# T5-bias attention followed by a mixture of adapters: a third of the adapter outputs taken from VectorE, the adapters' weights moved to the sync queue, later inputs loaded by token tiles

## The chip, the core and the metric

The kernel runs on one core of one Trainium2 chip. A core has TensorE (PE, matmuls; its weight loads are shown as PEld), VectorE (DVE), ScalarE (ACT), GpSimd (POOL) and SyncE (SP), each with an instruction stream of its own that runs in order, and 16 DMA engines that serve the queues of SP, ACT and POOL. The metric is the device time of one execution in microseconds, the median over runs.

## What is computed

`q`, `k` and `v` are [8, 8, 576, 64] in fp32 (batch, head, token, dimension). Attention with a T5 position bias gives 8 x 576 = 4608 tokens of 512 numbers. Each token then goes through the two of eight rank-16 adapters that its gate picks, and the result is added to it.

```python
scores = scale * np.matmul(q, k.transpose(0, 1, 3, 2)) + bias   # bias by distance, from a table
attn = softmax(scores)
x = np.matmul(attn, v)            # to [4608, 512]

logits = x @ w_gate               # [4608, 8]
w = softmax over the two largest logits of each token
delta = sum over those two e of w[e] * ((x @ A[e]) @ B[e])
return x + delta
```

## The kernel before

**Units and slots.** The work is cut into 32 units, one for each batch `b` and pair of heads `hp` (four pairs), numbered `u = 4b + hp`. A unit has six slots `s` (0 to 5). A loop over all 192 slots (line 586) writes the instructions of all engines in program order; each engine keeps that order, so an instruction that waits holds up all that stand behind it on its engine. In each slot `scores(u, s)` writes PE's score matmuls into one of two PSUM buffers and ACT's exponential that reads them (lines 256 and 260; line 268 for the last 64 keys). The value matmuls of the unit before (`values`, line 303), the bias multiplications on DVE (`bias`, lines 274 and 285) and, in slot 5, the normalisation on DVE (`normalise`, lines 313 and 314) follow.

**Inputs.** `load(b)` makes a list of DMA issues for one batch: fp32 staging tiles `q32`, `k32`, `v32` ([128 tokens, 4 token tiles, 8 heads, 64]) for tokens 0 to 511, and `qke32`, `ve32` for the last 64 tokens. There are two sets of staging tiles, used by batches in turn. A main load is one head: four token tiles, 128 KB, in pieces of 256 bytes. That makes 28 issues a batch, ordered by pair of heads. The loop pops them from the list onto SP's queue (line 595): three a slot in units 0 and 1, then one or two. The list for batch `b + 2` is made in slot 4 of pair 2 of batch `b` (line 646).

POOL casts the staged data to bf16. For unit `u + 2`, `cast_qk` (line 129) casts q in slot 2 and k in slot 4 of unit `u`; `cast_v` (line 133) casts v of unit `u + 1` in slot 1; `cast_tails` (lines 138 and 139) casts the last tokens of batch `b + 1` in slot 5 of pair 2. PE transposes the q and k of unit `u + 1` (`transpose_pe`, line 224) in slot 0 of unit `u` from unit 4 on, and DVE copies them out (line 228).

**Adapters' weights.** `load_adapters(c)` (line 202) issues six DMAs from POOL in the six slots of unit 3: four 128-row chunks of A and the gate into `AW` (bf16), and B into `Bc` (bf16). The DMA casts from fp32. They are first used by the `zl` matmuls (line 355).

**Adapters.** When a batch's attention is done, `batch_done` puts its token tiles into groups of three (of two for batch 6; batch 7 has a path of its own, class `Last`). A `Group` runs in steps, each a PE part and a part on other engines, which `place` spreads over even slots (slots 0, 2 and 4; slot 5 too in the last two batches): transposes of x, the z matmul and its copy on ACT, the gates on DVE, POOL and ACT, the transposes of the weighted z, and for each token tile `t` the output `dl_pe(t)` and `dl_out(t)`. `dl_out` is DVE's addition of x (line 407) and the store on SP's queue (line 409). `dl` takes one of the two PSUM buffers named `mm`, which the transposes use too. In a queue of steps, the output of tile 1 is followed by `weigh` of the next group (lines 381 to 387).

Of the kernel before, what the change touches and what calls it, by code (L numbers as in the profile page):

```python
# [11 lines left out]
FP32 = mybir.dt.float32  # L12
BF16 = mybir.dt.bfloat16
AX = mybir.AxisListType
ALU = mybir.AluOpType
# [18 lines left out]
def kernel(  # L34
# [11 lines left out]
    nc = tc.nc  # L46
    B, H, S, D = q.shape
    NB = bias_table.shape[0]
    Dm = H * D
    E = moe_w_gate.shape[1]  # L50
    r = moe_A.shape[2]
    ER = E * r
    HP = H // 2
# [15 lines left out]
    cp = ctx.enter_context(tc.tile_pool(name="const", bufs=1))  # L69
# [19 lines left out]
    def load(b):  # L89

        q32 = stg.tile([128, 4, H, D], FP32, name="q32", tag="q32")
        k32 = stg.tile([128, 4, H, D], FP32, name="k32", tag="k32")
        v32 = stg.tile([128, 4, H, D], FP32, name="v32", tag="v32")
        qke32 = stg.tile([128, H, D], FP32, name="qke32", tag="qke32")
        ve32 = stg.tile([128, HP, D], FP32, name="ve32", tag="ve32")
        staged[b] = (q32, k32, v32, qke32, ve32)
        todo = []

        def main(eng, t, src, hp):
            for h in (2 * hp, 2 * hp + 1):  # L100
                todo.append(lambda h=h: eng.dma_start(  # L101
                    out=t[:, :, h, :],
                    in_=src[b, h, :512, :].rearrange("(j p) d -> p j d", p=128)))

        for hp in range(HP):
            second = nc.scalar if b == 0 and hp == 0 else nc.sync
            main(nc.sync, q32, q, hp)
            main(second, k32, k, hp)
            if hp == 0:
                for i, (src, eng) in enumerate(((q, nc.sync), (k, second))):  # L110
                    todo.append(lambda i=i, src=src, eng=eng: eng.dma_start(
                        out=qke32[i * 64:(i + 1) * 64],
                        in_=src[b, :, 512:, :].rearrange("h p d -> p h d")))
            main(nc.sync, v32, v, hp)
            if hp == 0:
                for par in range(2):
                    todo.append(lambda par=par: nc.sync.dma_start(
                        out=ve32[par * 64:(par + 1) * 64],
                        in_=v[b, :, 512:, :].rearrange("(g two) p d -> two p g d", two=2)[par]))
        return deque(todo)  # L120
# [10 lines left out]
    def cast_v(u, eng):  # L131
        b, hp = units[u]
        eng(out=vals[b % 2][0][:, :, 2 * hp:2 * hp + 2, :D],  # L133
            in_=staged[b][2][:, :, 2 * hp:2 * hp + 2, :])
# [52 lines left out]
    ident = cp.tile([128, 128], BF16, tag="ident")  # L187
# [3 lines left out]
    todo = load(0)  # L191
# [7 lines left out]
    AW = cp.tile([128, 4, ER + E], BF16, tag="AW")  # L199
    Bc = cp.tile([ER, Dm], BF16, tag="Bc")  # L200

    def load_adapters(c):
        if c < 4:
            nc.gpsimd.dma_start(out=AW[:, c, :ER].rearrange("p (e r) -> p e r", e=E),
                                in_=moe_A[:, c * 128:(c + 1) * 128, :].rearrange("e d r -> d e r"))
        elif c == 4:
            nc.gpsimd.dma_start(out=AW[:, :, ER:], in_=moe_w_gate.rearrange("(c p) e -> p c e", p=128))
        else:
            nc.gpsimd.dma_start(out=Bc, in_=moe_B.rearrange("e r d -> (e r) d"))


    xs, xe, probs, accs = {}, {}, {}, {}
# [7 lines left out]
    def transpose_pe(u):  # L220
        ps = tps[u] = mp.tile([128, 2, 4, 128], BF16, name="tp", tag="mm")
        for i in range(2):
            for j in range(4):
                nc.tensor.transpose(ps[:, i, j, :], nats[u][:, i, j, :], ident)  # L224
# [15 lines left out]
    def scores(u, s):  # L240
        b, hp = units[u]
        qT, kT = qkT[b][:, hp, 0, :], qkT[b][:, hp, 1, :]
        sc = scp.tile([128, 2, SW], FP32, name="sc", tag="sc")
        if s == 0:
            probs[u] = (ep.tile([128, 2, 4 * S], BF16, name="pm", tag="pm"),
                        ep.tile([128, S], BF16, name="pe", tag="pe"))
        pm, pe = probs[u]
        if s < SLOTS - 1:
            c, end = SW * s, min(SW * (s + 1), 4 * S)
            n = end - c  # L250
            while c < end:
                j, q0 = divmod(c, S)
                w = min(S - q0, end - c)
                for h in range(2):
                    rows = slice(h * 64, (h + 1) * 64)
                    nc.tensor.matmul(sc[:, h, c - SW * s:c - SW * s + w],  # L256
                                     lhsT=kT[rows, j * 128:(j + 1) * 128],
                                     rhs=qT[rows, q0:q0 + w], start=True, stop=True)
                c += w
            nc.scalar.activation(pm[:, :, SW * s:end], sc[:, :, :n], ACT.Exp, scale=scale)  # L260
        else:
            flat = sc.rearrange("p a b -> p (a b)")
            for q0, n in ((0, 512), (512, 64)):
                for h in range(2):
                    rows = slice(h * 64, (h + 1) * 64)
                    nc.tensor.matmul(flat[rows, q0:q0 + n], lhsT=kT[rows, 512:],  # L266
                                     rhs=qT[rows, q0:q0 + n], start=True, stop=True)
            nc.scalar.activation(pe, flat[:, :S], ACT.Exp, scale=scale)  # L268
# [62 lines left out]
    class Group:  # L331
# [67 lines left out]
            nc.vector.tensor_copy(self.zT, self.zps)  # L399

        def dl_pe(self, t):
            self.dl = mp.tile([128, Dm], FP32, name="dl", tag="mm")
            nc.tensor.matmul(self.dl, lhsT=self.zT[:, t, :], rhs=Bc, start=True, stop=True)  # L403

        def dl_out(self, t):
            ot = ms.tile([128, Dm], FP32, name="ot", tag="ot", bufs=4)
            nc.vector.tensor_tensor(ot, self.dl, self.x[t], op=ALU.add)  # L407
            for p0, n0, cnt in self.rows[t]:
                nc.sync.dma_start(out=out[n0:n0 + cnt, :], in_=ot[p0:p0 + cnt, :])

# [175 lines left out]
    for t in range(SLOTS * NU):  # L586
        u, s = divmod(t, SLOTS)
        b, hp = units[u]
        p = u - 1
        scores(u, s)  # L590
        for fn, args in due.pop(t, []):
            fn(*args)
        if u == 3:
            load_adapters(s)
        for i in range(3 if u < 2 else 2 if s % 3 == 0 else 1):
            if loading:
                loading.popleft()()
        early = u >= NU - HP and hp in (0, HP - 1)
        if s == 0:
            if u == 0:  # L600
                while loading:
                    loading.popleft()()
                loading = load(1)
            if p >= 0:
                bias(p, 3)
                if not early:
                    values(p, 0)
            if HP <= u < NU - 1:
                transpose_pe(u + 1)
            place(t + 1)  # L610
        if s == 1:
            if p >= 0:
                bias(p, 4)
                values(p, 1)
            if u + 1 < NU:
                if u >= HP:
                    transpose_out(u + 1)
                cast_v(u + 1, pool_cast)
        if s == 2:
            if p >= 0:  # L620
                values(p, 2)
                if early:
                    values(p, 3)
            if u + 2 < NU:
                cast_qk(u + 2, 0, pool_cast)
            place(t + 1)
        if s == 3:
            if p >= 0:
                values(p, 4 if early else 3)
            bias(u, 0)  # L630
            if early:
                finish(p, t)
        if s == 4:
            if p >= 0 and not early:
                values(p, 4)
            if u + 2 < NU:
                cast_qk(u + 2, 1, pool_cast)
            if u < HP:
                transpose_pe(u + 1)
            if hp == HP - 1 and b + 1 < B:  # L640
                tails_pe(b + 1)
                tails_out(b + 1)
            if hp == 2 and b + 2 < B:
                while loading:
                    loading.popleft()()
                loading = load(b + 2)
            place(t + 1)
        if s == 5:
            if u < HP:
                transpose_out(u + 1)  # L650
            if p >= 0 and not early:
                finish(p, t)
            if hp == 2 and b + 1 < B:
                cast_tails(b + 1, pool_cast)
            bias(u, 1, 2)
            if u in (NU - HP - 1, NU - 2, NU - 1):
                values(u, 0)
            if b >= B - 2:
                place(t + 1)


    u = NU - 1
# [50 lines left out]
```

## Time and profile before

| what | value |
|---|---|
| median of 3 runs | 231.32 us (231.14 to 232.71) |
| the profiled execution's own time | 233.92 us |
| its span in the profile | 231.8 us |
| mean granted TensorE clock | 0.955 |
| loads of q, k, v by head: issues on SP and ACT, median to landing | 192 of 128 KB, 2.9 to 3.1 us |
| adapters' DMAs on POOL (lines 204, 207, 209) | 6 |
| output additions on DVE (line 407) | 31, of 0.68 us |
| copies of the same size from PSUM on ACT (line 561) | 3, of 0.586 us |
| packets of the sync queue, of POOL's queue | 120056, 4832 |

The profile is of one execution. Its page gives each engine's busy time, 40 equal slices of the span, and the DMA queues; other views list instructions in order of time with the idle time of the engine before each and what ended it, the chain of waits that ends with the last instruction, and busy times by stretch. An engine's busy time leaves out its waits and the issuing of DMAs.

### The profile page before, as it was taken

The page shows a single profiled execution, that of the slowest core. Times are in us where ns is not written, and L with a number is a line of the kernel's source. Part 1 is how long each engine was busy: PE and PEld are TensorE (multiplying, and loading weights), DVE is VectorE, ACT ScalarE, POOL GpSimd, SP SyncE. Part 2 cuts the span into 40 slices and gives each one's busy share as a digit, 9 for nine tenths or more (in the row PEclk, how much of TensorE's full clock was granted, in tenths as well). Part 3 has the DMA queues.
Part 4 walks back from the last instruction along what each step waited for, and adds up shares of the span by engine and source line. Part 5 has one row for each costly group of instructions (what it writes and reads, how often), then busy time and mean ns, then how long its engine had stood idle before and what let it go on. Part 6 is the DMA issues. An engine that isn't in the chain of part 4 may idle for free.

```text
span 231.8 us, 7224 instructions
## 1 busy us (share of the span) xinstructions
PE 181.6 (78%) x2900; PEld 121.7 (52%) x2900; DVE 174.9 (75%) x401; ACT 174.0 (75%) x225; POOL 97.1 (42%) x171
## 2 busy tenths in 40 slices
PE   0797857989899976888899976897888887796661
PEld 0354534666566663564566664565565655464530
DVE  5346763878798869787998869987988788987760
ACT  3587954999899876879789876897988767877422
POOL 2316497249413613805903613916507443411010
PEclk9999985999999999899999999999999999999955
DMA  7899899878879998797597785976597122222206
GB/s 163 199 244 221 188 161 208 186 165 202 196 170 234 223 247 203 208 246 184 137 229 185 210 201 146 251 172 173 114 230 214 48 77 73 90 48 95 90 29 199
DMA packets 126521, 39.74 MB, mean 171 GB/s; under 512 B 120464, under 2 KB 121880, under 8 KB 126488
## 3 DMA queue, kind: packets, MB, share of 16 engines
q1 hardware_dynamic: 120056, 38.62, 68.2%
q0 software_dynamic: 4832, 0.27, 3.5%
q10 hardware_dynamic: 1600, 0.40, 0.8%
q8 instruction: 22, 0.36, 0.6%
q14 instruction: 11, 0.09, 0.1%
HBM read 29.84 MB, written 9.45 MB: 169 GB/s over the span
## 4 chain that ended last, share of the span: by engine, by line
DVE 36%; PE 34%; ACT 8%; SPq 8%; issue 6%; DMA 4%; POOL 2%; POOLq 0%; ACTq 0%
DVE pm L285 12%; PE pv L303 11%; PE sc L256 9%; DVE xn L314 7%; ACT pm L260 7%; DVE ot L407 6%; SPq L101 5%; PE dl L403 2%; PE xT_ps L342 2%; DVE xT L347 2%; DVE rc L313 2%; PE tp L224 2%; PE zl L355 2%; DMA q<-in_q_dram 2%; DVE qkT L237 1%
## 5 line engine op out<-in xcount | busy, mean ns | idle before, releaser
L260 ACT ACTIVATE pm<-sc 128x1024 bf16<-128x1024 f32 (+1 forms) x160 | 142.2, 939 | 31.2 <-PE sc L256 30.2
L303 PE MATMUL pv<-vm,pm 128*128 128x65 bf16 x1280 | 63.0, 197 | 9.2 <-DVE xn L314 9.1
L285 DVE TENSOR_TENSOR pm<-pm,eb 128x512 bf16<-128x512 bf16 (+2 forms) x96 | 67.6, 725 | 2.4 <-DMA eb<-gx_d 1.9
L303 PEld LDWEIGHTS <-pm 128*128 128x128 bf16 x1280 | 51.2, 99 | 33.8 <-issue 20.7
L256 PE MATMUL sc<-qkT 64*128 64x384 bf16 (+7 forms) x512 | 61.9, 300 | 4.7 <-ACT pm L260 1.8
L370 POOL TENSOR_TENSOR ls<-z,top 128x24 f32<-128x24 f32 (+1 forms) x11 | 4.1, 372 | 66.1 <-DVE top L368 57.5
L256 PEld LDWEIGHTS <-qkT 64*128 64x128 bf16 x512 | 19.2, 95 | 20.8 <-issue 6.6
L224 PE MATMUL tp<-ident,qkn 128*128 128x128 bf16 x256 | 21.1, 227 | 10.5 <-DVE qkn L129 5.6
L228 DVE COPY qkT<-tp 128x1024 bf16<-128x1024 bf16 x32 | 21.9, 683 | 8.9 <-PE tp L224 8.9
L314 DVE TENSOR_TENSOR xn<-pv,rc 128x640 bf16<-128x640 f32 x32 | 26.4, 824 | 1.1
L133 POOL CAST vm<-v 128x512 bf16<-128x512 f32 x32 | 22.1, 690 | 10.3 <-DMA v<-in_v_dram 10.3
L129 POOL CAST qkn<-q 128x512 bf16<-128x512 f32 x30 | 23.1, 771 | 3.0 <-DMA q<-in_q_dram 1.5
L129 POOL CAST qkn<-k 128x512 bf16<-128x512 f32 x32 | 20.9, 652 | 6.6 <-DMA k<-in_k_dram 6.5
L268 ACT ACTIVATE pe<-sc 128x576 bf16<-128x576 f32 x32 | 20.8, 650 | 3.2 <-PE sc L266 2.2
L224 PEld LDWEIGHTS <-qkn 128*128 128x128 bf16 x256 | 15.9, 101 | 11.8 <-DVE qkn L129 5.6
L407 DVE TENSOR_TENSOR ot<-dl,xn 128x512 f32<-128x512 f32 x28 | 19.1, 683 | 2.8 <-PE dl L403 2.8
L266 PE MATMUL sc<-qkT 64*64 64x64 bf16 (+1 forms) x128 | 14.1, 294 | 7.5 <-ACT pm L260 7.3
L403 PE MATMUL dl<-Bc,zT 128*128 128x512 bf16 x31 | 12.2, 393 | 4.3 <-DVE ot L407 3.7
L313 DVE RECIPROCAL rc<-pv 128x10 f32<-128x10 f32 x32 | 6.9, 215 | 10.2 <-PE pv L303 10.2
L347 DVE COPY xT<-xT_ps 128x1024 bf16<-128x1024 bf16 (+1 forms) x20 | 11.2, 562 | 1.2 <-PE xT_ps L342 1.2
L266 PEld LDWEIGHTS <-qkT 64*64 64x64 bf16 x128 | 6.7, 105 | 9.3 <-issue 6.8
L385 POOL TENSOR_TENSOR gate<-nu,rd 128x24 f32<-128x24 f32 (+1 forms) x11 | 2.6, 239 | 19.4 <-DVE rd L383 8.7
(87 smaller groups left out, 164.8 us busy)
## 6 DMA issues: line engine op xcount, KB each, us to landing
q<-in_q_dram SPq DMA_DIRECT2D x64, 128.0 KB, 3.1
v<-in_v_dram SPq DMA_DIRECT2D x64, 128.0 KB, 2.9
k<-in_k_dram SPq DMA_DIRECT2D x62, 128.0 KB, 2.9
out_dram<-ot SPq DMA_DIRECT2D x28, 256.0 KB, 2.2
qke<-in_q_dram SPq DMA_DIRECT2D x8, 128.0 KB, 2.8
ve<-in_v_dram SPq DMA_DIRECT2D x16, 64.0 KB, 2.6
out_dram<-otL SPq DMA_DIRECT2D x4, 256.0 KB, 2.0
qke<-in_k_dram SPq DMA_DIRECT2D x7, 128.0 KB, 2.8
```

Source lines behind the costliest of these rows:

```text
L129: eng(out=nats[u][:, i].rearrange("p j (h d) -> p j h d", h=2), in_=src)
L133: eng(out=vals[b % 2][0][:, :, 2 * hp:2 * hp + 2, :D], in_=staged[b][2][:, :, 2 * hp:2 * hp + 2, :])
L224: nc.tensor.transpose(ps[:, i, j, :], nats[u][:, i, j, :], ident)
L228: nc.vector.tensor_copy(batch_tiles(b)[:, hp, :, :512], tps.pop(u).rearrange("p i j t -> p i (j t)"))
L256: nc.tensor.matmul(sc[:, h, c - SW * s:c - SW * s + w], lhsT=kT[rows, j * 128:(j + 1) * 128], rhs=qT[rows, q0:q0 + w], start=True, stop=True)
L260: nc.scalar.activation(pm[:, :, SW * s:end], sc[:, :, :n], ACT.Exp, scale=scale)
L266: nc.tensor.matmul(flat[rows, q0:q0 + n], lhsT=kT[rows, 512:], rhs=qT[rows, q0:q0 + n], start=True, stop=True)
L268: nc.scalar.activation(pe, flat[:, :S], ACT.Exp, scale=scale)
L285: nc.vector.tensor_tensor(t, t, e, op=ALU.mult)
L303: nc.tensor.matmul(pv[:, h, t * W:(t + 1) * W], lhsT=lhsT, rhs=rhs, start=(j == 0 and t == 0), stop=(j == 4), skip_group_check=True)
L314: nc.vector.tensor_tensor(_ap(xs[b], hp * 128, [[D, 2], [Dm, 5], [1, D]]), _ap(pv, 0, [[512, 2], [W, 5], [1, D]]), _ap(rc, 0, [[5, 2], [1, ...
L407: nc.vector.tensor_tensor(ot, self.dl, self.x[t], op=ALU.add)
```

## The change

Three things are changed.

The loads of batches 2 to 7 are cut by token tile: `rows(t, src, j)` loads token tile `j` of all eight heads in one DMA of 256 KB. The order is q and k of tiles 0 to 3 in turn, then the last tokens of q and k, then the four tiles of v, then the last tokens of v: 16 issues a batch. From batch 1 on the loop pops one a slot.

The adapters' weights are loaded in fp32 by SP's queue, in the six slots of unit 2, into new tiles `Af`, `Gf` and `Bf`. POOL casts them to `AW` and `Bc` in slots 1, 3 and 5 of unit 4; in slot 1 the cast stands ahead of `cast_v`.

In each group of three the output of tile 1 gets x from PE: a second matmul adds the identity times x to `dl`, ACT copies `dl` to the output tile, and DVE has no part in it. There are nine such groups.

```diff
+        def rows(t, src, j):
+            todo.append(lambda: nc.sync.dma_start(
+                out=t[:, j, :, :],
+                in_=src[b, :, j * 128:(j + 1) * 128, :].rearrange("h p d -> p h d")))
+
+        if b > 1:
+            for j in range(4):
+                rows(q32, q, j)
+                rows(k32, k, j)
-        for hp in range(HP):
+        for hp in range(HP if b < 2 else 1):
             second = nc.scalar if b == 0 and hp == 0 else nc.sync
-            main(nc.sync, q32, q, hp)
-            main(second, k32, k, hp)
+            if b < 2:
+                main(nc.sync, q32, q, hp)
+                main(second, k32, k, hp)
...
-            main(nc.sync, v32, v, hp)
+            if b < 2:
+                main(nc.sync, v32, v, hp)
+            else:
+                for j in range(4):
+                    rows(v32, v, j)
...
+    Af = cp.tile([128, 4, ER], FP32, tag="Af")
+    Gf = cp.tile([128, 4, E], FP32, tag="Gf")
+    Bf = cp.tile([ER, Dm], FP32, tag="Bf")
+
     def load_adapters(c):
         if c < 4:
-            nc.gpsimd.dma_start(out=AW[:, c, :ER].rearrange("p (e r) -> p e r", e=E),
-                                in_=moe_A[:, c * 128:(c + 1) * 128, :].rearrange("e d r -> d e r"))
+            nc.sync.dma_start(out=Af[:, c, :].rearrange("p (e r) -> p e r", e=E),
+                              in_=moe_A[:, c * 128:(c + 1) * 128, :].rearrange("e d r -> d e r"))
         elif c == 4:
-            nc.gpsimd.dma_start(out=AW[:, :, ER:], in_=moe_w_gate.rearrange("(c p) e -> p c e", p=128))
+            nc.sync.dma_start(out=Gf, in_=moe_w_gate.rearrange("(c p) e -> p c e", p=128))
         else:
-            nc.gpsimd.dma_start(out=Bc, in_=moe_B.rearrange("e r d -> (e r) d"))
+            nc.sync.dma_start(out=Bf, in_=moe_B.rearrange("e r d -> (e r) d"))
+
+    def cast_adapters(i):
+        out, src = ((AW[:, :, :ER], Af), (AW[:, :, ER:], Gf), (Bc, Bf))[i]
+        nc.gpsimd.tensor_copy(out=out, in_=src)
...
         def dl_pe(self, t):
             self.dl = mp.tile([128, Dm], FP32, name="dl", tag="mm")
-            nc.tensor.matmul(self.dl, lhsT=self.zT[:, t, :], rhs=Bc, start=True, stop=True)
+            own = t == 1 and self.n == 3
+            nc.tensor.matmul(self.dl, lhsT=self.zT[:, t, :], rhs=Bc, start=True, stop=not own,
+                             skip_group_check=True)
+            if own:
+                nc.tensor.matmul(self.dl, lhsT=ident, rhs=self.x[t], start=False, stop=True,
+                                 skip_group_check=True)
 
         def dl_out(self, t):
             ot = ms.tile([128, Dm], FP32, name="ot", tag="ot", bufs=4)
-            nc.vector.tensor_tensor(ot, self.dl, self.x[t], op=ALU.add)
+            if t == 1 and self.n == 3:
+                nc.scalar.copy(ot, self.dl)
+            else:
+                nc.vector.tensor_tensor(ot, self.dl, self.x[t], op=ALU.add)
...
-        if u == 3:
+        if u == 2:
             load_adapters(s)
-        for i in range(3 if u < 2 else 2 if s % 3 == 0 else 1):
+        if u == 4 and s % 2:
+            cast_adapters(s // 2)
+        for i in range(3 if u < 2 else 2 if s % 3 == 0 and b == 0 else 1):
```

## The prediction

> **What bounds the kernel now.** I read the page first: the busy shares, and the slices for the clock and the DMA engines.
>
> ```profile
> PE 181.6 (78%) x2900; PEld 121.7 (52%) x2900; DVE 174.9 (75%) x401; ACT 174.0 (75%) x225; POOL 97.1 (42%) x171
> ...
> PEclk9999985999999999899999999999999999999955
> DMA  7899899878879998797597785976597122222206
> ```
>
> No engine is full. The DMA engines are 70 to 90% busy until the loads end at about 180 us, and slice 6 (34.8 to 40.6 us) ran at half clock. So there are two stages to price: a start that waits for loads, and a middle in which three engines share the work. The table of stretches gives the middle (columns: window, length, then PE, PEld, DVE, ACT, POOL busy with counts, clock, DMA share, GB/s):
>
> ```profile
> 121.34:171.86 50.52, 42.35 (x724) 29.25 (x724) 43.03 (x96) 42.17 (x55) 22.13 (x38) 1.00 0.75 185
> ```
>
> This is one round of eight units (two batches). DVE, PE and ACT are busy 85, 84 and 83%: they are balanced, so less work on one of them pays only where the chain of waits runs through it. For the start I read the timeline of POOL, ACT and PE from 28 to 44 us (columns: start, length, engine, line, operation, idle time before it and its releaser):
>
> ```profile
> 33.15 0.79 POOL L129 CAST qkn<-q 128x512 bf16<-128x512 f32 x1
> 33.89 0.87 POOL L204 DMA_DIRECT2D AW<-in_moe_A_dram  x1
> 34.76 0.76 POOL L207 DMA_DIRECT2D AW<-in_moe_w_gate_dram  x1
> 35.50 0.63 POOL L129 CAST qkn<-k 128x512 bf16<-128x512 f32 x1
> 36.05 0.55 POOL L209 DMA_DIRECT2D Bc<-in_moe_B_dram  x1
> 36.59 0.63 POOL L133 CAST vm<-v 128x512 bf16<-128x512 f32 x1
> 37.14 0.63 POOL L129 CAST qkn<-q 128x512 bf16<-128x512 f32 x1
> 37.70 0.62 POOL L129 CAST qkn<-k 128x512 bf16<-128x512 f32 x1
> ```
> ```profile
> 37.38 1.02 ACT L260 ACTIVATE pm<-sc 128x1024 bf16<-128x1024 f32 x1 [4.24 <-PE sc L256]
> ```
> ```profile
> 36.19 0.61 PE L224 MATMUL tp<-ident,qkn 128*128 128x128 bf16 x4 [1.58 <-POOL qkn L129]
> 42.29 0.61 PE L224 MATMUL tp<-ident,qkn 128*128 128x128 bf16 x8
> ```
>
> POOL issues the adapters' DMAs between the casts of unit 5; PE's transposes of unit 5 wait for the k cast, and ACT stands idle 4.24 us behind PE. At 42.29 the transposes of unit 6 find their casts (37.14, 37.70) long done. Last, SP's timeline, since the adapters move into it:
>
> ```profile
> 28.26 2.24 SPq L101 DMA_DIRECT2D k<-in_k_dram  x2
> 30.54 1.11 SPq L101 DMA_DIRECT2D v<-in_v_dram  x2
> ...
> 38.98 1.90 SPq L101 DMA_DIRECT2D v<-in_v_dram  x2
> 40.98 0.99 SPq L101 DMA_DIRECT2D q<-in_q_dram  x2
> ```
>
> SP runs ahead of the engines; in the first 41 us only the DMAs hold it up. Batch 1's last load leaves it at 40.9 us, while the engines are in unit 4.
>
> **The change, part by part.**
>
> *Adapters off POOL.* Gone are 4 x 0.93 + 0.76 + 0.55 = 5.0 us of POOL between 29.78 and 36.6, and their traffic, during which SP's 16 loads from 28.26 on took 12.6 us (0.79 each). Unit 5's k cast could then start when k lands: issued by about 30, 2.9 us to landing (the page's median for k), so near 32.9 instead of 35.50. That removes about 3.0 us of ACT's 4.24 (bounds 2.0 and 4.2). Where it goes comes next.
>
> *Adapters on SP.* In the order of the built program the six loads stand on SP behind all of batch 1's loads and ahead of batch 2's, and each load on SP waits for the one eight before it to land. Batch 1's end: 16 issues from 28.26 at 0.55 to 0.67 each (pairs of 1.11 to 1.33 us) puts it at 37.1 to 38.9; I take 38.2. The four A loads have 1024 pieces of 64 bytes each. Lower bound 0.53 us each, the issue of any load; upper bound 1.7, at the software queue's time per packet now (3.5% of 16 x 231.8 us over 4832 packets is 27 ns; 64 packets a DMA engine). I take 1.0, nearer the sync queue's 21 ns per packet (68.2% over 120056) for smaller packets. With 2.0 us to landing (the output stores; 2.9 as upper bound) all of A is there at 38.2 + 4.0 + 2.0 = 44.2 us, bounds 41.2 and 48.6.
>
> The Trainium skill, "DMA: Bandwidth & Descriptors", section "Anatomy of one DMA", fits 2.0 us plus bytes/436e3 us per DMA, from DMAs that GpSimd issued. By it four loads of 64 KB would, as an estimate, land at 38.2 + 0.6 + 2.0 = 40.8 us, and the next paragraph's delay would be 0.8 us instead of 4.2; the page's "Specifications" speak against that fit here, as they name 512 bytes as the least piece for full rate.
>
> *The casts on POOL.* cast_adapters(0) stands in POOL's order right after unit 5's k cast (done near 33.5) and waits for all four A loads. Queued behind it: unit 5's v cast, unit 6's q cast, the gate's cast, unit 6's k cast (Bc's cast comes after that, ahead of a v cast that nobody waits for soon). From 44.2: 0.65 (the k cast's mean for 128x512) + 0.56 + 0.56 (start to start of casts above) + 0.25 (between 0.15, the memset, and 0.40, the ve cast) + 0.62 = 46.8 us for unit 6's k. Its four transposes started at about 42.6 before (second half of the row at 42.29). PE runs in order, so scores of unit 6 and all behind them are late by 46.8 - 42.6 = 4.2 us, bounds 1.2 and 8.6. The 3.0 us won at unit 5 is spent in this wait, not on top of it: PE now comes to unit 6 at 39 and stands there 7 us. The half clock that followed the wait at 33 to 36 follows this one instead: I take nothing for it, with 1 us as upper bound (ten pv matmuls 0.73 instead of 0.48 us over five slots, less what ACT's 1.02 us exponentials hide).
>
> *Batch 2 by token tiles.* The same bytes in 12 loads of 256 KB and 4 small ones instead of 28. A unit's first cast now needs all four tiles. Gate and B add 1.1 us, so they start on SP at 43.3. At 1.1 us each (two issues of 0.53 as lower bound, 64 packets x 21 ns = 1.35 as upper) the eighth leaves at 52.1 and lands near 55; unit 8's q cast ran at 50.50 and is due at 54.7 after the shift: covered within 0.3. ve lands at 43.3 + 12 x 1.1 + 4 x 0.62 + 0.5 (xe) + 2.6 = 62.1. POOL then has 0.40 + 3 x 0.56 before unit 9's k is done, 64.2, against transposes of unit 9 at 58.97 (second half 59.4) before: 4.8 us, bounds 1 and 11. It is one delay with the first (the larger counts): **+4.8**. For later batches the 16 loads take 16 of 24 slots, and their last landing has more than 5 us to spare.
>
> *Outputs t = 1.* Nine adds leave DVE (0.683, start to start 0.60). By their place (just before L381's reduction) six of the nine are pieces of the chain of waits, at 76.2, 108.3, 128.3, 159.0, 179.6 and 200.5, where each counts 0.60: -3.6; all nine would give -5.4. PE gets nine 512-column matmuls: 0.23 each (eight 128-column ones in 0.62 us are 57 ns apart) to 0.39 (dl's row), 2.1 to 3.5 us. ACT gets nine copies of 0.586 (L561's row), queued ahead of an exponential each; in the window above ACT waits 7.0 us for PE's scores, which covers 1.8 us of copies. A third of the new PE time, 2.4, counts (PE's share of the chain is 34%) and a sixth of ACT's 5.3: -3.6 + 0.8 + 0.8 = **-2.0**, bounds -5.4 and +3.
>
> Sum: 233.92 + 4.8 - 2.0 = 236.7 for the profiled execution (span 231.8 and 2.1 around it). The median of the runs is 2.6 below that execution, so 231.3 + 2.8 = **234.1 us**.
>
> **The rivals.** (1) Faster: A lands before POOL needs it. Then the 3.0 us at unit 5 stays won: 231.3 - 3.0 - 2.0 = 226.3. It decides if A is down by about 37 us, ahead of batch 1's end in SP's order (37.1 at the earliest); partial cases reach 229. For it: SP has no wait but DMAs. Against it: eight DMAs in flight in order of issue. (2) ACT becomes the bound: copies ahead of the exponentials, no time won on DVE: 231.3 + 4.8 + 5.3 = 241.4. For it: ACT is busy 83% and would be 87. Against: DVE falls from 85 to 81. (3) The two terms cancel, at the low end of the landing and the high end of DVE's gain: 231.3 + 3 - 3.5 = 230.8, no change.
>
> **How the numbers follow.** Forecast 0.52 (own range 232 to 238), rival 1 0.18, rival 2 0.12, rival 3 0.18. About 1% is what a measurement here can tell from no change: 229.0 and 233.6. Faster: rival 1 and little else, 0.19. Same: rival 3 and the low part of the forecast, 0.29. Slower: 0.52. The range 228 to 240 leaves out most of rival 1 and half of rival 2.
>
> **What would show it.** On POOL at 34 to 44 us one wait for DMA Af at the first adapters' cast, and PE's transposes of unit 6 waiting for POOL's qkn; unit 5's no longer. DVE at 169 us busy, ACT at 179. Wrong if that cast waits under 3 us, if ve of batch 2 lands after 66, or if DVE's idle time grows by what it lost in work.

## The result, and the profile after

The changed kernel takes **241.81 us** (median of 4 runs, 238.89 to 242.54) against 231.90 us for the kernel before on the same chip (4 runs): a ratio of 1.0385, interval [1.0278, 1.0492]. It is 9.9 us slower by the medians; the prediction said 2.8 us slower, and its range ended at 240. The ratio goes by the fast runs alone (one of the four, 242.54 us, fell in a slower state with a clock of 0.937), and by it the loss is 8.9 us. The profiled execution took 242.18 us, with a span of 239.9 us and a mean granted clock of 0.949.

The page of after, its busy times and the slices for the clock and the DMA engines:

```profile
PE 185.7 (77%) x2909; PEld 123.0 (51%) x2909; DVE 166.9 (70%) x392; ACT 177.9 (74%) x234; POOL 94.2 (39%) x168
...
PEclk9997699769979999999999999999999999999967
DMA  8999989799999589997679399993995303132206
```

DVE lost 8.0 us of work, ACT gained 3.9 and PE 4.1 (169 and 179 us were forecast for DVE and ACT). The slices tell where to look: up to 90 us before had one place near half clock, slice 6; after has three, slices 3 and 4, 7 and 8, and 11, counted from 0 and 6.0 us long. The first leaves no delay at the end of unit 4 (-0.3 us in the table below); the other two stand at the waits that follow here. From slice 12 to the end of the attention all are at full clock.

The round of eight units that corresponds to the one shown of before (columns as there):

```profile
130.26:181.15 50.89, 42.94 (x727) 29.28 (x727) 40.96 (x93) 43.42 (x59) 22.42 (x38) 1.00 0.89 192
```

50.89 us against 50.52: DVE works 2.1 us less in it and nothing is faster. So the loss lies ahead of it. The timeline of POOL (start, length, engine, line, operation, idle time before it and its releaser):

```profile
33.92 0.62 POOL L143 CAST qkn<-k 128x512 bf16<-128x512 f32 x1 [0.89 <-DMA k<-in_k_dram]
46.12 0.62 POOL L231 CAST AW<-Af 128x512 bf16<-128x512 f32 x1 [11.58 <-DMA Af<-in_moe_A_dram]
...
47.23 0.62 POOL L143 CAST qkn<-q 128x512 bf16<-128x512 f32 x1
...
47.95 0.62 POOL L143 CAST qkn<-k 128x512 bf16<-128x512 f32 x1
...
65.04 0.40 POOL L153 CAST ve<-ve 128x256 bf16<-128x256 f32 x1 [4.30 <-DMA ve<-in_v_dram]
65.38 0.62 POOL L147 CAST vm<-v 128x512 bf16<-128x512 f32 x1
65.94 1.40 POOL L143 CAST qkn<-q 128x512 bf16<-128x512 f32 x1
67.29 0.87 POOL L143 CAST qkn<-k 128x512 bf16<-128x512 f32 x1
```

Unit 5's k is cast at 33.92, no longer at 35.50. The next cast is that of the adapters, and POOL waits 11.58 us for it, with unit 6's q and k queued behind. Twenty us later POOL waits again, for the last tokens of batch 2, with unit 9's q and k behind. On ACT and PE:

```profile
37.68 3.35 ACT L282 ACTIVATE pm<-sc 128x1024 bf16<-128x1024 f32 x4 [0.83 <-PE sc L278]
49.80 1.02 ACT L282 ACTIVATE pm<-sc 128x1024 bf16<-128x1024 f32 x1 [7.19 <-PE sc L278]
```
```profile
47.91 1.32 PE L246 MATMUL tp<-ident,qkn 128*128 128x128 bf16 x8 [6.03 <-POOL qkn L143]
68.21 0.40 PE L246 MATMUL tp<-ident,qkn 128*128 128x128 bf16 x4 [0.42 <-POOL qkn L143]
```

ACT's wait of 4.24 us in unit 4 has shrunk to 0.83, and one of 7.19 stands in its place a unit later. PE's transposes of unit 6 come at 47.91 instead of 42.29, the second half of unit 9's at 68.21 instead of 59.20 (the fifth of the eight matmuls that start at 58.97 in before). The chain of waits runs through both places (start, length, what):

```profile
41.14 2.33 SPq L222
...
43.52 2.45 DMA Af<-in_moe_A_dram
...
62.28 2.61 DMA ve<-in_v_dram
```

And SP, which hands out both loads (the first row is the pair of k that leaves at 28.26 in before):

```profile
29.89 1.05 SPq L101 DMA_DIRECT2D k<-in_k_dram  x2
...
39.95 4.15 SPq L222 DMA_DIRECT2D Af<-in_moe_A_dram  x4
44.14 0.58 SPq L225 DMA_DIRECT2D Gf<-in_moe_w_gate_dram  x1
44.77 0.50 SPq L227 DMA_DIRECT2D Bf<-in_moe_B_dram  x1
45.38 0.37 SPq L106 DMA_DIRECT2D q<-in_q_dram  x1
...
62.28 0.61 SPq L131 DMA_DIRECT2D ve<-in_v_dram  x1
```

### The profile page after: what moved, and what is told of

Its sections match the earlier page's. It is cut to its first block, busy times and chain, and to the rows that moved or that the text cites. A ratio compares the mean times of both kernels' runs of the same rounds, so it can differ in the third digit from the quotient of the medians.

```text
span 239.9 us, 7135 instructions
## 1 busy us (share of the span) xinstructions
PE 185.7 (77%) x2909; PEld 123.0 (51%) x2909; DVE 166.9 (70%) x392; ACT 177.9 (74%) x234; POOL 94.2 (39%) x168
## 4 chain that ended last, share of the span: by engine, by line
DVE 32%; PE 32%; SPq 13%; ACT 8%; issue 5%; DMA 5%; POOL 3%; POOLq 0%
DVE pm L307 12%; PE pv L325 10%; SPq L101 10%; PE sc L278 8%; ACT pm L282 6%; DVE xn L336 6%; DVE ot L438 4%; PE xT_ps L364 2%; PE dl L427 2%; DVE xT L369 2%; DVE rc L335 2%; PE zl L377 2%; PE tp L246 2%; SPq L222 1%; DMA gx_d<-gxe 1%
## 5 line engine op out<-in xcount | busy, mean ns | idle before, releaser
L325 PE MATMUL pv<-vm,pm 128*128 128x65 bf16 x1280 | 63.7, 198 | 7.1 <-DVE xn L336 7.1
L307 DVE TENSOR_TENSOR pm<-pm,eb 128x512 bf16<-128x512 bf16 (+2 forms) x96 | 65.0, 698 | 2.4 <-DMA eb<-gx_d 2.0
L278 PE MATMUL sc<-qkT 64*128 64x384 bf16 (+7 forms) x512 | 62.8, 304 | 4.5 <-ACT pm L282 1.9
L143 POOL CAST qkn<-q 128x512 bf16<-128x512 f32 x30 | 23.8, 795 | 3.3 <-DMA q<-in_q_dram 3.0
L438 DVE TENSOR_TENSOR ot<-dl,xn 128x512 f32<-128x512 f32 x19 | 13.0, 685 | 3.3 <-PE dl L427 3.3
L259 DVE COPY qkT<-tpe 128x512 bf16<-128x512 bf16 x8 | 3.4, 425 | 12.2 <-PE tpe L256 12.2
```

The source lines that it names most:

```text
L143: eng(out=nats[u][:, i].rearrange("p j (h d) -> p j h d", h=2), in_=src)
L278: nc.tensor.matmul(sc[:, h, c - SW * s:c - SW * s + w], lhsT=kT[rows, j * 128:(j + 1) * 128], rhs=qT[rows, q0:q0 + w], start=True, stop=True)
L307: nc.vector.tensor_tensor(t, t, e, op=ALU.mult)
L325: nc.tensor.matmul(pv[:, h, t * W:(t + 1) * W], lhsT=lhsT, rhs=rhs, start=(j == 0 and t == 0), stop=(j == 4), skip_group_check=True)
```

## The experiments

To compare runs unit by unit I take from each trace the end of a unit's exponential over the last 64 keys (line 268 of the kernel before). In the profile of before these stand at 42.0 (unit 4), 58.4 (7), 64.0 (8), 88.7 (12) and 193.1 us (28). The table shows how much later each run reaches them, and the ratio of its runs to those of the kernel before on the same chip. A trace is one execution: the differences at unit 4, up to 1.8 us, arise ahead of both waits, and from unit 12 to 28 the profile of before holds a phase at half clock, at 92 us, that most others lack (104.4 us from unit 12 to unit 28, against 102.9 in g3). So the table tells where a loss arises, and the ratio how large it is.

```text
run                        u4    u7    u8   u12   u28   ratio, interval
after                    -0.3  +7.4  +9.7 +10.2  +9.7   1.0385 [1.0278, 1.0492]
e1 adapters back on POOL +0.1  +0.7  +4.3  +4.9  +4.8   1.0143 [1.0095, 1.0192]
e2 adapters only         -0.2  +7.3  +7.3  +7.3  +5.9   1.0279 [1.0227, 1.0330]
e3 outputs only          -1.1  -1.4  -1.4  -1.1  -1.2   0.9974 [0.9929, 1.0019]
e4 token tiles only      +0.3  +0.3  +1.3  +1.3  +1.3   1.0153 [1.0076, 1.0230]
f1 tiles, ve ahead of v  -1.2  -0.5  +4.3  +4.5  +3.1   1.0138 [1.0074, 1.0203]
f2 after, casts later    -0.3  +7.3  +9.8 +10.4  +9.8   1.0402 [1.0340, 1.0464]
f3 adapters in batch 1   +1.8  +1.6  +1.6  +1.6  +0.1   0.9999 [0.9961, 1.0037]
f4 no t = 1 additions    -0.9  -1.1  -1.1  -1.6  -3.9   0.9849 [0.9772, 0.9926]
g2 heads, need-last      -0.1  +0.5  +4.7  +5.0  +3.4   1.0214 [1.0153, 1.0275]
g3 e2, casts later       -0.5  -0.4  -0.4  -0.3  -1.8   1.0004 [0.9968, 1.0040]
g4 ACT copy, POOL add    +0.6  +0.6  +0.6  +1.0  +1.0   1.0026 [0.9979, 1.0074]
h1 both orders undone    -1.1  +0.7  +0.7  +1.4  +0.8   0.9997 [0.9965, 1.0030]
h2 ACT copy, no addition -1.0  -1.3  -1.3  -1.3  -3.6   0.9881 [0.9850, 0.9912]
```

**One part at a time.** e1 is the changed kernel with the adapters' lines of before; e2, e3 and e4 are the kernel before with one part of the change each, taken from the diff above.

```diff
# e1, against the changed kernel
-            nc.sync.dma_start(out=Af[:, c, :].rearrange("p (e r) -> p e r", e=E),
...
+            nc.gpsimd.dma_start(out=AW[:, c, :ER].rearrange("p (e r) -> p e r", e=E),
...
-        if u == 2:
+        if u == 3:
             load_adapters(s)
-        if u == 4 and s % 2:
-            cast_adapters(s // 2)
```

> The changed kernel with the adapters' loads back on POOL in unit 3, as before the change; token tiles and ScalarE outputs stay. Theory (the first adapters' cast on POOL waits 11.6 us behind batch 1's loads and holds unit 6's casts): 231 to 234 us, ACT's 7.2 us wait in unit 5 gone, the 4.2 us wait in unit 4 back. Rival (the token tiles or the ScalarE copies cost the time): 237 to 241 us.

> The kernel before with the adapters' part alone (SP loads in unit 2, POOL casts in unit 4). Theory: 235 to 238 us, POOL's first adapters' cast waits about 11 us for DMA. Rival: 230 to 232.5 us.

> The kernel before with the t = 1 outputs alone on PE and ACT. The prediction's term: 229 to 230 us (-2.0). Theory from the changed kernel's round of eight units (50.9 us against 50.5): 231 to 232.5 us, no gain. Rival (ACT becomes the bound): 235 us or more.

> The kernel before with the loads of batches 2 to 7 by token tiles alone. Theory: 231 to 233 us, since without the adapters ahead of them on SP batch 2's loads land some 5 us earlier than in the changed kernel and POOL's wait for ve of batch 2 shrinks from 4.3 us to 2 or less. Rival (the tiles are what costs): 236 us or more.

Measured: e1 236.22, e2 239.36, e3 232.18, e4 237.18 us, against 232.56. By the ratios of the table the adapters' part alone costs 6.5 us (2.8%), token tiles alone 3.6 (1.5%), and the outputs alone are worth 0.6 (0.3%, its interval holds no change). The table separates the two losses: e2 has lost everything by unit 7, e1 nearly everything at unit 8. e4's profiled execution was the fastest of its four and shows a loss of 1.3 only; the wait that costs is to be read in e1, on POOL and PE:

```profile
52.02 0.62 POOL L143 CAST qkn<-q 128x512 bf16<-128x512 f32 x1 [1.45 <-DMA q<-in_q_dram]
52.93 1.35 POOL L143 CAST qkn<-k 128x512 bf16<-128x512 f32 x1 [0.29 <-DMA k<-in_k_dram]
...
58.88 0.40 POOL L153 CAST ve<-ve 128x256 bf16<-128x256 f32 x1 [2.50 <-DMA ve<-in_v_dram]
```
```profile
62.10 0.61 PE L238 MATMUL tp<-ident,qkn 128*128 128x128 bf16 x4 [0.18 <-POOL qkn L143]
```

In before the same two casts found their data, and unit 9's transposes ran at 58.97:

```profile
50.50 0.61 POOL L129 CAST qkn<-q 128x512 bf16<-128x512 f32 x1
...
53.26 1.13 POOL L139 CAST ve<-ve 128x256 bf16<-128x256 f32 x1
```
```profile
58.97 0.61 PE L224 MATMUL tp<-ident,qkn 128*128 128x128 bf16 x8
```

Unit 8's q, which needs the fourth q tile, and ve, the last load of the batch, are both late in e1, without any adapters on SP.

**Is it ve alone?** f1 is e4 with ve's two loads put ahead of v's tiles.

```diff
+            if b > 1:
+                for par in range(2):
+                    todo.append(lambda par=par: nc.sync.dma_start(
+                        out=ve32[par * 64:(par + 1) * 64],
...
-            if hp == 0:
+            if hp == 0 and b < 2:
```

> Token tiles alone, with the two loads of v's last tokens moved ahead of v's four tiles. Theory (the tiles cost their time because POOL stands at the cast of batch 2's ve until the whole batch has landed, 4.0 us in the run with tiles alone, and unit 9's casts stand behind it): back to 231 to 233.5 us, POOL's wait for ve under 1 us. Rival (256 KB loads are themselves what costs, by holding SP's stores or filling the DMA engines): it stays at 236 to 238 us.

Measured: 235.76 us against 232.34 (1.0138), as slow as e4. ve's wait is gone and v's has come in its place:

```profile
60.40 0.62 POOL L152 CAST vm<-v 128x512 bf16<-128x512 f32 x1 [4.86 <-DMA v<-in_v_dram]
```

With token tiles the first pair's v needs every v load of the batch. The theory that ve is the whole matter falls.

**The adapters' casts moved behind unit 7's k.** f2 does it to the changed kernel, g3 to e2.

```diff
-        if u == 4 and s % 2:
-            cast_adapters(s // 2)
...
+            if u == 5:
+                for i in range(3):
+                    cast_adapters(i)
```

> The changed kernel with the three casts of the adapters' weights moved on POOL from unit 4 (slots 1, 3, 5) to unit 5, slot 4, behind unit 7's k cast; loads stay where they are. Theory (order on POOL): unit 6's casts no longer wait for Af, ACT's 7.2 us wait in unit 5 goes, the z matmul of the first group waits for AW until about 47.5 us instead, up to 4 us: 236 to 239 us. Rival (the loads' place on SP or their traffic is what costs, wherever the cast stands): 241 to 242 us.

> Kernel before with the adapters' part of the change alone (fp32 on the sync queue in unit 2, loads by head kept), the three casts on POOL moved from slots 1, 3 and 5 of unit 4 to slot 4 of unit 5, behind unit 7's k cast. Theory (where batch 2 comes by head, only the place of the casts in POOL's order costs: unit 6's q and k casts stood behind them): 232 to 234.5 us, unit 6's casts without a wait. Rival (the adapters' place on the sync queue, ahead of batch 2, costs by itself): 237 to 239.5 us, with the casts of unit 8 waiting for DMA q.

Measured: f2 241.74 us against 232.34 (1.0402), no better than the changed kernel; g3 232.93 against 232.77 (1.0004). The same edit is worth 6.4 us (239.36 to 232.93) in one kernel and nothing in the other. In f2 unit 6 is free of its wait, and POOL stands at unit 8 instead:

```profile
45.66 0.61 POOL L231 CAST AW<-Af 128x512 bf16<-128x512 f32 x1 [3.15 <-DMA Af<-in_moe_A_dram]
...
56.83 0.61 POOL L143 CAST qkn<-q 128x512 bf16<-128x512 f32 x1 [6.47 <-DMA q<-in_q_dram]
```

In g3, where batch 2 comes by head, the same cast runs at 50.08 without a wait, though SP hands out the same six adapter loads ahead of it. So the adapters' 5.4 us on SP (39.95 to 45.38) cost nothing in sum by themselves; they cost where POOL has a cast queued behind them, or where a cast needs the end of the batch that follows them.

**Size of the loads or order of need?** g2 keeps 128 KB heads and takes the order of token tiles: what the first pair needs comes last.

```diff
+        if b > 1:
+            for h in reversed(range(H)):
+                head(q32, q, h)
+                head(k32, k, h)
...
+            for h in reversed(range(H)):
+                head(v32, v, h)
```

> Kernel before, but the loads of batches 2 to 7 stay single heads of 128 KB and are put in the order that token tiles have: all heads of q and k (heads 7 to 0), the last tokens, all heads of v (7 to 0), the last tokens of v. So unit 8's casts need the last q and k loads and the last v load of the batch, as with token tiles, while size and number of the loads are those of before. Theory (what token tiles cost is the order of need: one pair's cast waits for the whole batch): 235 to 237.5 us, POOL's q or v cast of unit 8 waits over 2 us for a DMA. Rival (the 256 KB loads themselves are slower, the order is covered): 231.5 to 233 us, no such wait.

Measured: 237.53 us against 232.77 (1.0214), no faster than e4. The timeline of POOL in g2:

```profile
51.92 0.61 POOL L149 CAST qkn<-q 128x512 bf16<-128x512 f32 x1 [1.61 <-DMA q<-in_q_dram]
...
60.73 0.40 POOL L159 CAST ve<-ve 128x256 bf16<-128x256 f32 x1 [4.62 <-DMA ve<-in_v_dram]
```

The wait of token tiles appears without one token tile. The order of need costs; that the 256 KB loads cost besides is not seen.

**Adapters ahead of need.** f3 is e2 with the six loads between q, k and v of batch 1's third pair, and the casts in slots 0, 1 and 5 of unit 5.

```diff
+            if b == 1 and hp == 2:
+                todo += [lambda c=c: load_adapters(c) for c in range(6)]
...
-        if u == 4 and s % 2:
-            cast_adapters(s // 2)
+        if u == 5 and s in (0, 1, 5):
+            cast_adapters((0, 1, 5).index(s))
```

> The kernel before with the adapters loaded in fp32 by SP, but among batch 1's loads (behind q and k of its third pair of heads), and cast on POOL in unit 5, slots 0, 1 and 5. Theory: A lands near 41 us, ahead of its cast, POOL issues nothing, and unit 4's stall of 4.2 us is gone with no new one above 2 us: 228 to 230.5 us. Rival (the start is bound by the DMA engines whatever the order): 231 to 234 us.

Measured: 232.31 us against 232.34 (0.9999), no change. Neither here nor in g3 does POOL issue the adapters' DMAs any more, and nothing is won over before: the end of unit 3 stands at 37.5 us in f3 and at 35.1 in g3, against 31.6 in before, so what POOL's DMAs cost in unit 4 is lost ahead of it (the next section says where this begins).

**Both orders undone, the rest of the change kept.** h1 is g3 with the change's outputs.

> The changed kernel with its two orders undone: loads of batches 2 to 7 by head and pair as before (the token tiles are gone), and the adapters' casts on POOL in slot 4 of unit 5, behind unit 7's k cast. The adapters stay in fp32 on the sync queue in unit 2, and the outputs of tile 1 stay on PE and ACT. Theory (the whole loss of the change is the two orders, what stands behind what in the start; nothing is left of it in the rest): 231 to 233.5 us, no difference from before. Rival (the outputs on PE and ACT or the fp32 adapters cost where the parts meet): 235 to 238 us.

Measured: 232.96 us against 233.02 (0.9997). With the adapters in fp32 on SP and the outputs on PE and ACT, but without the two orders, nothing of the loss is left: of 3.85% remains none, within 0.35%. One wait that the change brought is still in its trace: PE's first z matmul waits 2.21 us for the late cast of A, at 47.67.

**What the outputs are worth.** f4 leaves the nine additions out and stores a tile of zeros, h2 has ACT's copies in their place (x is not added), g4 ACT's copies and POOL's additions in SBUF.

```diff
-            nc.vector.tensor_tensor(ot, self.dl, self.x[t], op=ALU.add)
+            if t == 1 and self.n == 3:
+                ot = zero                                               # f4
+                nc.scalar.copy(ot, self.dl)                             # h2, g4
+                nc.gpsimd.tensor_tensor(ot, ot, self.x[t], op=ALU.add)  # g4
+            else:
+                nc.vector.tensor_tensor(ot, self.dl, self.x[t], op=ALU.add)
```

> The kernel before without the nine t = 1 additions: DVE does nothing for them and a tile of zeros is stored, so those output rows are left out. It gives what freeing DVE alone is worth. Prediction's term before its costs on PE and ACT: -3.6, so 228 to 229.5 us; then PE's matmuls and ACT's copies gave it back. Rival (DVE does not set the pace, the waits move to PE and ACT): 230.5 to 232.5 us, as with the outputs part alone.

> Kernel before with the nine outputs of tile 1 copied by ACT alone: neither DVE nor PE nor POOL adds x, and these rows of the output hold delta without x. It stands between the run without the nine outputs' additions (228.56 us) and the one with both PE's matmuls and ACT's copies (232.18 us). If PE's matmuls gave back what DVE won: 228.5 to 229.8 us. If ACT's copies did: 231 to 232.5 us. In between: both.

> Kernel before with the nine outputs of tile 1 taken from DVE in another way: ACT copies dl out of PSUM, POOL adds x to the copy in SBUF; PE has no second matmul. If PE's matmuls gave back what DVE won: 229 to 230.5 us. If ACT's copies did, or there is nothing to win: 231.5 to 233 us.

Measured: f4 228.56 us against 232.34 (0.9849), h2 230.33 against 233.02 (0.9881), g4 233.86 against 232.77 (1.0026). Taking the additions off DVE is worth 1.5%, 3.5 us. ACT's copies give back 0.3%, 0.7 us, which the intervals don't resolve. From h2 to e3, that is with PE's nine matmuls added, 0.9% is given back, 2.2 us, and these intervals lie apart. POOL's additions cost more still, 1.5% from h2 to g4, and there POOL queues its additions behind ACT's copies (17.5 us of waiting in eight places). PE's new matmuls in e3 (group of the costliest instructions: count, busy us, mean ns):

```profile
L408 PE MATMUL dl<-xn,ident 128*128 128x512 bf16 x9 | 3.7, 407 | 0.0
```

None of the runs that compute the whole output beats the kernel before by more than its interval.

## Why the prediction was wrong

The direction and the path were right: POOL's one wait for Af at the first adapters' cast, PE's transposes of unit 6 behind it, unit 5's no longer held up by DMA issues, batch 2's end as the later of the two delays. The size was not. By its own steps:

*Adapters off POOL.* Half right. Unit 5's k was cast at 33.92, 1.6 us earlier (2.6 forecast), and ACT's wait fell from 4.24 to 0.83. But what was won there had been lost before, and was not spent in the next wait: unit 3 ended at 35.3 us instead of 31.6, unit 4 at 41.7 instead of 42.0, and PE came to unit 6 at 41.9 and stood 6.0 us (39 and 7 forecast). This is no accident of one execution. The pair of k that left SP at 28.26 in before leaves at 29.33 to 29.89 in the six traces whose adapters SP loads (after, e2, f2, f3, g3, h1), and at 27.85 to 28.47 in the nine whose POOL loads them. The difference is there at SP's first `eb` load already (8.99 to 9.26 us against 7.89 to 8.19), up to which SP's order is the same in all. The prediction put this late start at nothing; why it comes with the adapters' part, no run shows. Rival 1, that A comes before POOL needs it, falls with POOL's wait of 11.58 us.

*A landed.* 45.97 us (43.52 + 2.45) against 44.2. The time from the first issue came out, 4.15 us on SP (4.0) and 6.02 to the last landing (6.0), but by luck: not four loads of 1.0 us each, but three of 0.51 to 0.58, as a 128 KB head takes at that time, and one of 2.33. SP came to them at 39.95 instead of 38.2, 1.6 of it the late start (29.89 against 28.26); from there it took 10 us for 16 loads, as forecast. By the Trainium skill, "DMA: Bandwidth & Descriptors", "Anatomy of one DMA", the prediction estimated a landing at 40.8 us; from 39.95 on the same fit gives 42.6, an estimate too, and for these loads of 64-byte pieces the measured 45.97 decides against it.

*The delay at unit 6.* Forecast 4.2, measured 6.1 at the transposes (48.62 by the chain, against 42.51; the prediction had read 42.6) and 7.4 at the end of unit 7. The first difference is the 1.8 us by which A landed later. The second, 1.3, is the clock, priced at nothing with a bound of 1 us. The table of stretches shows it (columns as above):

```profile
41.90:47.90 6.00, 0.00 (x0) 0.00 (x0) 0.76 (x3) 0.72 (x1) 1.78 (x4) 0.74 0.79 119
47.90:51.67 3.77, 3.66 (x34) 2.37 (x34) 1.59 (x3) 1.02 (x1) 2.90 (x6) 0.50 1.23 229
```

PE does nothing for 6 us; when it resumes it is the bound, 3.66 of 3.77 us at half clock. The argument that ACT's exponentials hide slow matmuls failed because the exponentials had nothing to read yet: ACT waits for PE's scores at 49.80 and again, 1.02 us, at 51.85.

*Batch 2.* **This is the step that failed**: the term +4.8, with ve landed at 62.1 and unit 9's k cast by 64.2. Measured: 9.7 us at the end of unit 8. The term is mis-sized, in five pieces: batch 2 started on SP at 45.38 instead of 43.3 (2.1, of which 1.6 are the late start); from there to ve's landing at about 64.9 it took 19.5 us instead of 18.8 (0.7); POOL needed 3.3 us instead of 2.1 from there to the end of unit 9's k at 68.16, with casts of 1.40 and 0.87 us where 0.56 each was taken (1.2); the second half of unit 9's transposes stood at 59.20 in before, not at 59.4 (0.2); and 3.4 us at half clock behind them took 0.7 more. The sum, 4.9, is what 4.8 lacks to 9.7.

That no adapters would mean no delay here followed from the same sum, and is refuted: e1's ve cast begins at 58.88, unit 9's transposes are 2.9 us late (62.10 against 59.20), and half a clock for 6.8 us makes it 4.3 at unit 8. g2 shows that it is the order of need. That unit 8's q is "covered within 0.3" held only behind the first wait: f2, without it, waits 6.47 us there.

*One delay, the larger counts.* Right, and shown by f2: without the first wait (unit 6 on time) unit 8 is as late as with it, +9.8 against +9.7. That the parts alone, 6.5 + 3.6 - 0.6 = 9.5 by their ratios, come near to the whole loss (8.9 by its ratio) all the same agrees with SP's times: the adapters' 5.4 us there push back the whole of a batch that by its order is 4.3 late at unit 8 already (e1), and 5.4 + 4.3 is 9.7. No run takes this sum apart.

*Outputs.* DVE's -3.6 was right (f4: 3.5). ACT's +0.8 agrees with h2's 0.7. PE's +0.8 was too small by 1.4: nine matmuls of 0.41 us are 3.7 us of PE, and 2.2 of them count, not a third of 2.4. The forecast of -2.0 becomes -0.6, so with 9.7 the sum is 9.1, between the 8.9 us of the ratio and the 9.9 of the medians. The sign I had named for a failure here, DVE's idle time growing by what it lost in work, was there: 73.0 us in after against 56.9, which is its 8.0 us and the 8.1 of the longer span, and in e3, where no start is longer, 62.1, 5.2 of the 7.5 lost. Rival 3, that the two terms cancel, falls with 9.7 against -0.6. ACT as the bound (rival 2, with 241.4 close to the result) gets no support: the copies cost little, in e3 as in h2, and the loss is complete before the adapters' outputs begin.

## What to carry to other kernels

An in-order engine that prepares data should never have a step for a later need queued ahead of one for an earlier need: g3 and f2 change nothing but where three casts stand, and in g3, with no second wait behind, that is worth the whole 2.8%. Regrouping loads by a different axis changes the moment when the first consumer can start from "its own part landed" to "the last part landed", even when bytes and queue time are the same (g2); so price a load by the landing of the last piece that its first consumer needs. And add to every wait of TensorE that is expected to reach several microseconds the slow matmuls behind it, 0.7 to 1.4 us each here.

## What the runs showed of the hardware

**The clock.** Ahead of a span's last 20 us, half-clock phases lasted 3.4 or 6.8 us (10.2 in e3 and f2), and in after one began about 3 us into PE's gap: the gap ran from 41.9 to 47.9, the phase from 44.84 to 51.67. What it cost, from the transposes to the end of the unit: 1.3 us in after at unit 6, 1.4 in e1 at unit 9, 0.7 for a phase of 3.4 us in after at unit 9. The Trainium skill, "TensorE: Matmul & The Clock Gate", "What's actually happening", says that the gate goes by windows of about 3.4 us that run freely, to half rate after an idle one and back after a busy one; the phases agree in length. The cost of one phase is small, but a stalled start has several.

**POOL beside DVE.** The cast of 1.40 us at 65.94 in after (0.62 for most) stands beside DVE's multiplication of two tiles in SBUF, which is slow itself at that moment:

```profile
65.91 1.76 DVE L307 TENSOR_TENSOR pm<-pm,eb 128x1536 bf16<-128x1536 bf16 x2
```

Two such multiplications take 1.35 us together at 54.59, where POOL does nothing. The Trainium skill, "SBUF — State Buffer", "SBUF: two separate sides", says that DVE and GpSimd hold a shared pair of ports in turn, a DVE operation with two SBUF inputs among the holders. The pair of rows agrees with it; no run separated the two engines, so the cause stays argued.

**Small pieces.** Of the four A loads of 64-byte pieces three left SP in 0.51 to 0.58 us, as a 128 KB head does (0.51 at that time); the third took 2.33 us. In f3, where they stand among batch 1's loads, the third took 0.76 us, so the pieces alone do not make it slow. What held SP at it was not tried.
